# Own chunks first, weight loads in pairs over two rings, and the W_out casts on one engine: a change to the start of a convolution and GELU feed-forward kernel

## The chip, the cores and the metric

The kernel runs on one core of one Trainium2 chip. The metric is the device time of one execution in microseconds (us). The profile of a run shows a span that is about 1.7 us shorter than the run's time. Times below are medians of runs; positions inside a trace are us from the start of the span.

## The reference

Eight sequences of 4096 tokens with 192 channels go through a causal convolution of 7 taps. The taps are a softmax over a small weight table, one row for each of 8 heads of 24 channels. The result goes through a feed-forward layer with an exact GELU.

```python
def _attn_ref(x, weight):                 # x [8, 4096, 192], weight [8, 7]
    w = np.exp(weight - np.max(weight, axis=-1, keepdims=True))
    w = w / (np.sum(w, axis=-1, keepdims=True) + 1e-09)
    x_pad = np.concatenate([np.zeros((B, 6, D)), x], axis=1)
    ...                                   # idx: the 7 tokens that end at each token
    return np.einsum('hk,bskhg->bshg', w, x_unf).reshape(B, S, D)

def _moe_ref(x, w_in, w_out):             # w_in [192, 2048], w_out [2048, 192]
    h = x @ w_in
    g = 0.5 * h * (1.0 + erf(h * inv_sqrt2))
    return (g @ w_out).astype(np.float32)
```

## The kernel before

The 32768 tokens are split into two halves. Partitions 0 to 63 hold channels of half 0, partitions 64 to 127 those of half 1, so two products of 64 rows run side by side on TensorE (in the trace of this kernel the two of a pair start 3 ns apart at 32.14 us and take 269 ns each). Each half is cut into 35 blocks, of which the first six have 256 tokens and the others 512. Blocks 0 and 1 are convolved on TensorE, with diagonal tap matrices; VectorE convolves all later blocks. A small block is worked in 8 slices. A slice is 12 matmuls with W_in, one GELU of 1.02 us on ScalarE, and a share of the 128 matmuls with W_out that belong to the block before.

W_in arrives as float32. Half 0's partitions load the first 1024 columns and half 1's the last 1024. The "own" cast turns a group of 256 of these columns into bf16 on the partitions that loaded it. A "dup" copies a group to the other half's partitions, because each half of the tokens needs all 2048 columns. Loads are issued by SyncE (the "SP ring") and by ScalarE (the "ACT ring"); the page lists the two as queues q1 and q10, with 52.51 and 0.98 MB in this kernel.

```python
CH = []                                      # order of the 16 chunks of 128 columns, both halves alike
for s in range(4):
    CH += [2 * s, 2 * s + 1, NF // 2 + 2 * s, NF // 2 + 2 * s + 1]

def own(e, s):                               # f32 -> bf16, 128 partitions
    e.wait_ge(S_WIN[s], 32)
    ...
def dup(s, hf):                              # to the other half, 64 partitions, read from the f32 copy
    v.wait_ge(S_WIN[s], 32)
    ...
# VectorE, blocks 0 and 1
for p in range(NP):
    trans(0, p)
own(v, 0).then_inc(S_DUPE)
dup(0, 0)
conv_out(v, 0, 1)
conv_out(v, 0, 4)
dup(0, 1)
dup(1, 0)
dup(1, 1)
for p in range(NP):
    trans(1, p)
own(v, 2).then_inc(S_DUPE)
for s in (2, 3):
    for hf in range(2):
        dup(s, hf)
for j in range(len(PIECES)):
    conv_out(v, 1, j)
for i in range(2, 4):
    wcast(v, i).then_inc(S_WOC)

# TensorE, at the start of a slice of block 0
t.wait_ge(S_DUPE, (2, 3, 4, 5, 7, 8, 9, 10)[i])
t.wait_ge(S_OWN, sum(s <= i // 2 for s in OWNG))

# SP ring
load(sp, 0, (0, 1))
for s in range(2):
    win_in(sp, s, 0)                         # half 1 of these two groups goes out on ACT's ring
load(sp, 1)
for s in range(2, 4):
    for hf in range(2):
        win_in(sp, s, hf)
for i in range(4):
    wout_in(sp, i)
load(sp, 2)
```

## Time and profile before

| what | value |
|---|---|
| time, 3 runs | 687.38 us (687.08 to 687.88) |
| span of the profiled run | 684.6 us |
| TensorE busy | 675.7 us, 99% of the span |
| block 0's first product | 11.09 us |
| block 1's first product | 21.61 us |
| block 2's first product | 32.14 us |

Apart from the warm-up matmuls, TensorE does the same work in every version here, and from block 2 on it has no hole (busy for 645.7 of the 646 us from 34 to 680 us, before and after). So the time is the start of block 2's first product plus a constant: 684.6 − 32.14 = 652.5 us in this trace. Everything is decided in the first 33 us.

The timeline of TensorE in the kernel before shows how that time is spent. The columns are start, duration, engine, line, operation, tiles, shape and count; the bracket is the idle time before the group and what ended it.

```profile
11.09 4.51 PE L781 MATMUL hp<-xc,win 64*128 64x256 bf16 x48 [2.08 <-POOL win L226]
16.73 0.83 PE L781 MATMUL hp<-xc,win 64*128 64x256 bf16 x12 [1.13 <-ACT gT L703]
19.66 1.50 PE L781 MATMUL hp<-xc,win 64*128 64x256 bf16 x24
21.61 0.83 PE L781 MATMUL hp<-xc,win 64*128 64x256 bf16 x12 [0.45 <-ACT gT L703]
```

### The profile page before, as it was taken

The numbers are of one execution on the slowest core, as the hardware profiler recorded it, in microseconds if no ns is written. First come the engines' busy times: TensorE is split into PE (matmuls) and PEld (weight loads), VectorE is DVE, ScalarE is ACT, GpSimd is POOL, SyncE is SP. The second block draws the span as 40 slices with busy tenths as digits, with TensorE's granted clock in tenths as the row PEclk, the third lists the DMA queues.
The fourth block names the chain that finished last, engine by engine and source line by source line (L and its number), as shares of the span: only waits on it lengthen the run. The fifth ranks groups of instructions, "written<-read, shape, count | busy, mean of one in ns | idle before, by whom it ended". The sixth has DMA issues, their size and how long they took to land.

```text
span 684.6 us, 27324 instructions
## 1 busy us (share of the span) xinstructions
PE 675.7 (99%) x12576; PEld 408.9 (60%) x12576; DVE 564.1 (82%) x905; ACT 537.2 (78%) x550; POOL 35.9 (5%) x52
## 2 busy tenths in 40 slices
PE   6999999999999999999999999999999999999998
PEld 3899755555555555555555555555555555555557
DVE  6999989888898888898888898888898888988611
ACT  5899987877777877788777877777877777778772
POOL 3124200000000000000000000000000000000000
PEclk9999999999999999999999999999999999999999
DMA  9454421244422344422344322444322444221223
GB/s 231 87 116 109 103 60 35 62 94 95 94 60 59 73 94 95 93 57 53 83 94 95 88 51 56 91 94 95 81 48 63 95 94 95 69 48 29 48 49 94
DMA packets 134322, 55.23 MB, mean 81 GB/s; under 512 B 127552, under 2 KB 134208, under 8 KB 134208
## 3 DMA queue, kind: packets, MB, share of 16 engines
q1 hardware_dynamic: 132640, 52.51, 34.9%
q8 instruction: 98, 1.61, 1.0%
q10 hardware_dynamic: 1536, 0.98, 0.5%
q14 instruction: 16, 0.13, 0.1%
q0 software_dynamic: 32, 0.00, 0.0%
HBM read 28.31 MB, written 25.17 MB: 78 GB/s over the span
## 4 chain that ended last, share of the span: by engine, by line
PE 96%; ACT 2%; DMA 1%; issue 1%; DVE 0%; POOL 0%; ACTq 0%; POOLq 0%
PE hp L781 48%; PE ob L843 42%; PE ob L812 5%; ACT gT L703 2%; DMA winf<-in_moe_w_in_dram 1%; DMA wsb<-in_weight_dram 0%; PE ob L733 0%; ACT osb L301 0%; DVE osb L343 0%; POOL win L226 0%; DVE osb L312 0%; ACT L644 0%; ACT wex L637 0%; DVE wmx L490 0%; ACTq L238 0%
## 5 line engine op out<-in xcount | busy, mean ns | idle before, releaser
L703 ACT ACTIVATE gT<-hp 128x1024 bf16<-128x1024 f32 x512 | 523.4, 1024 | 131.5 <-PE hp L781 128.3
L781 PE MATMUL hp<-xc,win 64*64 64x512 bf16 (+2 forms) x6048 | 419.7, 367 | 3.8 <-POOL win L226 2.1
L843 PE MATMUL ob<-gT,wout 64*64 64x512 bf16 x5376 | 366.3, 376 | 0.0
L571 DVE SCALAR_TENSOR_TENSOR acc<-xT,wcol,acc 128x512 f32<-128x512 f32 (+1 forms) x495 | 314.6, 704 | 0.0
L781 PEld LDWEIGHTS hp<-xc,win 64*64 64x64 bf16 (+1 forms) x6048 | 189.0, 106 | 138.4 <-ACT gT L703 3.2
L843 PEld LDWEIGHTS ob<-gT,wout 64*64 64x64 bf16 x5376 | 172.2, 118 | 122.6
L343 DVE STREAM_TRANSPOSE osb<-ob 128x512 f32<-128x512 f32 x84 | 74.2, 886 | 102.0 <-PE ob L843 102.0
L538 DVE STREAM_TRANSPOSE xT<-xin 128x512 f32<-128x512 f32 (+1 forms) x105 | 78.0, 795 | 0.0
L571 DVE SCALAR_TENSOR_TENSOR xc<-xT,wcol,acc 128x512 bf16<-128x512 f32 (+1 forms) x99 | 65.2, 715 | 0.0
L471 POOL COPY xT<-xT 128x18 f32<-128x18 f32 x30 | 28.0, 934 | 509.0 <-DVE xT L538 486.6
L812 PE MATMUL ob<-wout,gT 64*128 64x192 bf16 x1024 | 51.8, 243 | 0.1
L812 PEld LDWEIGHTS ob<-wout,gT 64*128 64x128 bf16 x1024 | 43.7, 94 | 5.7 <-issue 0.4
L564 DVE TENSOR_SCALAR acc<-xT,wcol 128x512 f32<-128x512 f32 (+1 forms) x90 | 37.6, 474 | 1.1
L314 ACT ACTIVATE osb<-ob 128x192 f32<-128x192 f32 x4 | 1.3, 332 | 9.5 <-PE ob L812 9.5
L312 DVE COPY osb<-ob 128x192 f32<-128x192 f32 x4 | 1.4, 358 | 8.4 <-PE ob L812 8.4
L514 DVE CAST win<-winf 64x768 bf16<-64x768 f32 x8 | 6.6, 820 | 0.3
L717 PE MATMUL hp<-warm 128*128 128x512 bf16 x16 | 5.3, 505 | 1.3 <-DVE warm L487 1.3
L301 ACT ACTIVATE osb<-ob 128x384 f32<-128x384 f32 x12 | 5.8, 486 | 0.0
L676 ACT ACTIVATE acc<-xT,wcol 128x256 f32<-128x256 f32 (+1 forms) x9 | 5.2, 576 | 0.0
L717 PEld LDWEIGHTS hp<-warm 128*128 128x128 bf16 x16 | 1.9, 125 | 4.2 <-issue 2.2
L733 PE MATMUL ob<-xTb,dg 64*64 64x256 bf16 (+1 forms) x112 | 3.2, 245 | 0.8 <-ACT xTb L652 0.8
L733 PEld LDWEIGHTS ob<-xTb,dg 64*64 64x64 bf16 x112 | 2.6, 106 | 1.7 <-ACT xTb L652 1.3
(31 smaller groups left out, 21.3 us busy)
## 6 DMA issues: line engine op xcount, KB each, us to landing
out_dram<-osb SPq DMA_DIRECT2D x122, 192.0 KB, 3.6
xin<-in_x_dram SPq DMA_DIRECT2D x116, 192.0 KB, 4.2
xin<-in_x_dram SPq DMA_DIRECT2D x22, 96.0 KB, 3.9
woutf<-in_moe_w_out_dram SPq DMA_DIRECT2D x4, 384.0 KB, 7.5
winf<-in_moe_w_in_dram SPq DMA_DIRECT2D x6, 192.0 KB, 5.6
winf<-in_moe_w_in_dram ACTq DMA_DIRECT2D x2, 192.0 KB, 4.8
out_dram<-osb SPq DMA_DIRECT2D x8, 48.0 KB, 1.7
out_dram<-osb ACTq DMA_DIRECT2D x4, 96.0 KB, 2.0
```

What stands on the lines that cost most here:

```text
L343: v.transpose(ap(osb[m % 2], j, [[8 * C, 128], [C // 2, TB // 32], [NP, 32]]), bank(ring(m, j)),).then_inc(S_EV)
L471: g.tensor_copy(dst, src).then_inc(S_HALO)
L514: v.tensor_copy(ap(win, 64 * (1 - hf) * NP * F + FH + FP[s], [[NP * F, 64], [F, NP], [1, FP[s + 1] - FP[s]]],), ap(winf, 64 * hf * NP * FH ...
L538: v.transpose(ap(xT[n % 2], p * XW + HX, [[NP * XW, 128], [1, w]]), ap(xin[n % NX], p, [[TB // 32 * DQ, 128], [DQ, w // 32], [NP, 32]],),) ...
L564: ins = v.tensor_scalar(a, src, wk, None, ALU.mult)
L571: ins = v.scalar_tensor_tensor(dst, src, wk, a, op0=ALU.mult, op1=ALU.add)
L703: a.activation(out=ap(gT[n % 2], i * c * 2 * w, dst), in_=ap(hp[u % 2], 0, src), func=AF.Gelu,).then_inc(S_GELU)
L717: t.matmul(hp[1][:, 0:512], warm[:, 0:128], warm[:, :])
L733: ins = t.matmul(bank(kd, slice(64 * ho, 64 * ho + 64), w), dg[r, d0 : d0 + 64], xTb[PC[n]][r, x0 : x0 + w], start=(k == KS - 1), stop=(k ...
L781: ins = t.matmul(hp[u % 2][fo : fo + fw, o : o + w], ap(win, f1, [[NP * F, 64], [2, fw]]), xc[n % 2][r, p * TB : p * TB + w], start=(p == ...
L812: ins = t.matmul(bank(bb[sub], w=C), gT[m % 2][r, c0 : c0 + 128], wout[r, CH[i] * C : (CH[i] + 1) * C], start=(ph == 0 and i == 0), stop=( ...
L843: ins = t.matmul(bank(ring(m, j), slice(64 * h, 64 * h + 64), w), ap(wout, 64 * hf * NF * C + CH[i] * C + j, [[NF * C, 64], [NP, 64]],), g ...
```

## The change

The intent is to start TensorE earlier and to keep VectorE free for block 2.

1. Each half begins with the chunks of its own part of W_in: half 0 takes chunks 0 to 15, half 1 takes 8 to 15 and then 0 to 7. Slices 0 to 3 need only own casts, one on VectorE and three on GpSimd.
2. The dups read the bf16 copy, not the float32 one.
3. All W_in groups are loaded in pairs, half 0 on the SP ring and half 1 on ACT's ring, ahead of x block 1.
4. The softmax weights are loaded first on the SP ring, and no longer by GpSimd.
5. GpSimd casts all four pieces of W_out.
6. In block 1 the W_out matmuls are spread unevenly over the slices, and TensorE waits for the W_out casts at two named units (a unit is two W_out matmuls).

```diff
-    CH = []
-    for s in range(4):
-        CH += [2 * s, 2 * s + 1, NF // 2 + 2 * s, NF // 2 + 2 * s + 1]
+    CH = [[(8 * hf + i) % NF for i in range(NF)] for hf in range(2)]
 ... GpSimd
-            own(g, OWNG[0]).then_inc(S_OWN)
+            for s in range(1, 4):
+                own(g, s).then_inc(S_OWN)
             halo(1)
             for p in range(NP):
                 cast(g, 1, p)
-            own(g, OWNG[1]).then_inc(S_OWN)
-            for i in range(2):
+            for i in range(4):
                 wcast(g, i).then_inc(S_WOG)
 ... VectorE, in dup(s, hf)
-                v.wait_ge(S_WIN[s], 32)
+                if s == 0:
+                    v.wait_ge(S_DUPE, 1)
+                else:
+                    v.wait_ge(S_OWN, s)
 ...
-                        winf,
+                        win,
 ... VectorE
             own(v, 0).then_inc(S_DUPE)
-            dup(0, 0)
             conv_out(v, 0, 1)
             conv_out(v, 0, 4)
-            dup(0, 1)
-            dup(1, 0)
-            dup(1, 1)
+            for s in range(2):
+                for hf in range(2):
+                    dup(s, hf)
             for p in range(NP):
                 trans(1, p)
-            own(v, 2).then_inc(S_DUPE)
 ...
-            for i in range(2, 4):
-                wcast(v, i).then_inc(S_WOC)
 ... ScalarE
-            for s in range(2):
+            for s in range(4):
                 win_in(a, s, 1)
 ... TensorE
-                    t.wait_ge(S_DUPE, (2, 3, 4, 5, 7, 8, 9, 10)[i])
-                    t.wait_ge(S_OWN, sum(s <= i // 2 for s in OWNG))
+                    if 1 <= i < 4:
+                        t.wait_ge(S_OWN, i)
+                    else:
+                        t.wait_ge(S_DUPE, 1 if i == 0 else 2 * (i - 4) + 3)
 ...
+            share = {1: [4, 8, 8, 8, 9, 9, 9, 9]}
 ...
-                    ws = SHARE if new else [1] * NSL[n]
+                    ws = SHARE if new else share.get(n, [1] * NSL[n])
 ...
-                    if n == 1 and i < 2:
-                        t.wait_ge((S_WOG, S_WOC)[i], 2)
                     for un in todo[a0:a1]:
+                        if n == 1 and un in ((0, 0, 0), (0, 0, 4)):
+                            t.wait_ge(S_WOG, 2 + un[2] // 2)
 ... SP
+            sp.dma_start(wsb ...).then_inc(S_WSB, 16)     # taken from GpSimd
             load(sp, 0, (0, 1))
-            for s in range(2):
+            for s in range(4):
                 win_in(sp, s, 0)
             load(sp, 1)
-            for s in range(2, 4):
-                for hf in range(2):
-                    win_in(sp, s, hf)
```

More of the change, by code (lines that the diff above doesn't have):

```diff
@@ L152, in bass_lightweight_conv__then__act_gelu_exact_kernel @@
         S_OWN = sem("S_OWN")
-        S_WOC = sem("S_WOC")
         S_WOG = sem("S_WOG")
@@ L217, in bass_lightweight_conv__then__act_gelu_exact_kernel @@
         FP = [0, 256, 512, 768, FH]
-        OWNV = (0, 2)
-        OWNG = (1, 3)
         WG = [0, 4, 2, 6]
@@ L411, in _ @@
         def _(g):
-            g.dma_start(
-                wsb[:, :], ap(wt, 0, [[KS, H], [0, 64 // H], [1, KS]])
-            ).then_inc(S_WSB, 16)
             g.wait_ge(S_MSET, 1)
@@ L520, in dup @@
                     ap(
-                        winf,
-                        64 * hf * NP * FH + FP[s],
-                        [[NP * FH, 64], [FH, NP], [1, FP[s + 1] - FP[s]]],
+                        win,
+                        64 * hf * NP * F + FP[s],
+                        [[NP * F, 64], [F, NP], [1, FP[s + 1] - FP[s]]],
                     ),
@@ L594, in _ @@
             own(v, 0).then_inc(S_DUPE)
-            dup(0, 0)
             conv_out(v, 0, 1)
             conv_out(v, 0, 4)
-            dup(0, 1)
-            dup(1, 0)
-            dup(1, 1)
+            for s in range(2):
+                for hf in range(2):
+                    dup(s, hf)
             for p in range(NP):
                 trans(1, p)
-            own(v, 2).then_inc(S_DUPE)
-            for s in (2, 3):
+            for s in range(2, 4):
                 for hf in range(2):
@@ L766, in mm1 @@
                 if n == 0:
-                    t.wait_ge(S_DUPE, (2, 3, 4, 5, 7, 8, 9, 10)[i])
-                    t.wait_ge(S_OWN, sum(s <= i // 2 for s in OWNG))
+                    if 1 <= i < 4:
+                        t.wait_ge(S_OWN, i)
+                    else:
+                        t.wait_ge(S_DUPE, 1 if i == 0 else 2 * (i - 4) + 3)
                 for cc in range(c):
-                    f0 = 256 * (CH[i * c + cc] // 2) + CH[i * c + cc] % 2
                     for p in range(NP):
@@ L776, in mm1 @@
                             r = slice(64 * hf, 64 * hf + 64)
+                            ch = CH[hf][i * c + cc]
+                            f0 = 256 * (ch // 2) + ch % 2
                             fw = 64 if M0 < n <= M1 else 128
@@ L814, in mm2 @@
                         gT[m % 2][r, c0 : c0 + 128],
-                        wout[r, CH[i] * C : (CH[i] + 1) * C],
+                        wout[r, CH[sub][i] * C : (CH[sub][i] + 1) * C],
                         start=(ph == 0 and i == 0),
@@ L846, in mm2_t @@
                                 wout,
-                                64 * hf * NF * C + CH[i] * C + j,
+                                64 * hf * NF * C + CH[h][i] * C + j,
                                 [[NF * C, 64], [NP, 64]],
@@ L890, in _ @@
         def _(sp):
+            sp.dma_start(
+                wsb[:, :], ap(wt, 0, [[KS, H], [0, 64 // H], [1, KS]])
+            ).then_inc(S_WSB, 16)
             load(sp, 0, (0, 1))
-            for s in range(2):
+            for s in range(4):
                 win_in(sp, s, 0)
             load(sp, 1)
-            for s in range(2, 4):
-                for hf in range(2):
-                    win_in(sp, s, hf)
             for i in range(4):
```

## The prediction

> **What bounds the kernel now.** I read the busy times first, then the slices, then the first 35 us of the chain and of the engines' timelines.
>
> ```profile
> PE 675.7 (99%) x12576; PEld 408.9 (60%) x12576; DVE 564.1 (82%) x905; ACT 537.2 (78%) x550; POOL 35.9 (5%) x52
> ...
> PE   6999999999999999999999999999999999999998
> ...
> PEclk9999999999999999999999999999999999999999
> DMA  9454421244422344422344322444322444221223
> ```
>
> TensorE is busy for 99% of the span, at full granted clock, and only the first slice (17 us) has a hole. The change leaves the number and shape of matmuls alone, so it can only earn what TensorE loses at the start. The chain of waits shows that loss:
>
> ```profile
> 5.13 4.99 DMA winf<-in_moe_w_in_dram
> 10.12 0.05 issue
> 10.17 0.84 POOL win L226
> 11.01 0.09 issue
> 11.09 3.78 PE hp L781 x35
> ...
> 15.93 0.80 issue
> ...
> 21.61 0.83 PE hp L781 x12
> 22.44 0.66 PE ob L812 x16
> ```
>
> The first product with W_in (block 0) starts at 11.09 us, block 1's first product at 21.61. From there the stream has a period of 1.31 us per slice (12 matmuls with W_in, 16 with W_out) without a hole. The idle times in front of TensorE's instructions after the warm-up matmuls sum to 0.77 + 2.08 + 1.13 + 0.45 = 4.4 us; a stretch at reduced clock comes on top (granted clock 0.72 between 10 and 16 us). Note that the chain names GpSimd's cast of chunk 1 as the releaser at 11.09. The code says otherwise: the first slice waits for VectorE's duplicate (ended 10.53) and VectorE's copy of the convolution result (10.57 to 10.99), and that copy is the true releaser. Both sit behind VectorE's own cast, which waited for W_in until 9.13.
>
> VectorE has a second line to watch, since it computes the convolution for blocks 2 and on:
>
> ```profile
> 21.62 1.03 DVE L235 CAST wout<-woutf 128x768 bf16<-128x768 f32 x2
> 22.57 1.34 DVE L538 STREAM_TRANSPOSE xT<-xin 128x256 f32<-128x256 f32 x3
> ...
> 30.67 1.27 DVE L571 SCALAR_TENSOR_TENSOR xc<-xT,wcol,acc 128x256 bf16<-128x256 f32 x3
> ...
> 32.14 0.82 PE L781 MATMUL hp<-xc,win 64*128 64x256 bf16 x12
> ```
>
> VectorE works without a pause from 22.57 to 31.94 (9.4 us) on block 2, and TensorE takes that block at 32.14: a slack of 0.2 us. It is the same at block 3 (conv done 42.5, product at 42.66); from block 4 on, where ScalarE makes the first tap, the slack is 2 us and more. So **what TensorE gains before block 2 counts only as far as VectorE starts block 2 earlier too.** Two things hold that start: VectorE's earlier queue, and the landing of x block 2, whose last piece landed 9.3 us after an issue at 12.26, at 21.55.
>
> Last, what the DMA moved in three stretches (the last two columns are the share of the 16 engines and GB/s):
>
> ```profile
> 9.40:12.20 2.80, 1.11 (x14) 0.83 (x16) 2.67 (x6) 0.28 (x2) 0.98 (x2) 0.88 1.12 240
> 13.50:16.50 3.00, 2.10 (x26) 1.16 (x22) 2.97 (x5) 2.63 (x3) 2.51 (x5) 0.76 1.07 374
> 17.50:20.50 3.00, 3.00 (x86) 2.28 (x86) 2.84 (x6) 2.05 (x2) 0.84 (x2) 1.00 1.29 215
> ```
>
> The engines are saturated in all three, yet W_in pieces (64 partitions each, one after the other on one ring) move at 240 GB/s, W_out (128 partitions) at 374, x (32 partitions each) at 215.
>
> [...] from 4.4 to 5.0 us the SP ring wrote W_in to partitions 0 to 63 while the ACT ring finished x on 64 to 127, and 359 GB/s moved. That is one short stretch with mixed packet sizes. [...] The duplicates now read f32, and the shortest takes 684 ns for 768 elements; no bf16 copy is in this trace. [...] a duplicate takes 686 ns at the median and up to 1273 while GpSimd casts.
>
> **The change part by part.**
>
> *Softmax weights on the SP ring.* They land 2.8 us after a GpSimd issue at 1.32, at 4.13; issued first on SP at 0.81 I estimate 3.0, since the first 96 KB piece of x took 2.7 us. So the tap matrix is ready at about 5.2 instead of 6.34. x block 0 landed at 5.46 and its SP half now goes out 0.6 us later, so the transpose starts at about 5.5 instead of 6.25: 0.7 earlier. ScalarE's cast must stand behind four issues of 0.62 us from about 3.4 on, so it starts at about 6.0 instead of 6.86. The convolution on TensorE ends at about 8.2 instead of 9.0.
>
> *Own chunks first.* Slice 0 needs only one cast of chunk group 0 and no duplicate. Once the convolution copies are out (VectorE about 8.1) TensorE starts at about **8.4 instead of 11.09**. Slices 1 to 3 wait for GpSimd's three casts of 0.82 us.
>
> *Pairs over both rings.* Both halves of a chunk group fly together, ahead of x block 1. If the rate rises from 240 to 350 GB/s, W_in's 1.57 MB take 4.5 us instead of 6.5: groups land at about 6.5, 7.4, 8.4, 9.4 (x block 1 at about 11.2), and everything behind comes 2 us earlier. If not, they land at about 7.1, 8.7, 10.3, 11.9 and x block 1 where it landed before, 13.8.
>
> *Order of slices.* ScalarE's GELU takes 1.02 us, more than TensorE's 0.65 per slice, so slices follow at 1.03 us where weights allow. With the fast DMA: GELU of slice 0 at 9.2 to 10.2, slice 3 until 13.3. The four duplicates of groups 0 and 1 [...] and x block 1's transposes (1.35) end at about 13, the block-1 convolution on TensorE at 15.2, the last four duplicates at 15 to 16.6, VectorE's six copies (2.29 us) at 17.3 to 18.9. Block 1's first product then comes at **17.1 to 18.7 instead of 21.61**: 2.9 to 4.5 us gained on TensorE. With the slow DMA the same sum gives 19.7 to 20.6: 1.0 to 1.9.
>
> *W_out on GpSimd.* Four casts of 1.015 us from about 13.7 end at 17.7 to 19.6. They are needed after block 1's second slice (18.7 to 20.3), so they just fit. VectorE loses 1.03 us of casts before block 2.
>
> *VectorE's start of block 2.* It is the later of its copies (17.3 to 18.9) and x block 2. With the fast DMA I put x block 2 at 21.55 minus 2.4, so 19.1: 3.4 us earlier. With the slow DMA it lands at about 21.5, and the start moves from 22.57 to 21.6: 1.0 us.
>
> The gain is the smaller of the two lines: about **3.0 us** with the fast DMA (2.9 to 3.4), about **1.0 us** with the slow one. Steady state carries either shift unchanged to the end: its period is TensorE's own, and what is issued in it stays the same in number and shape.
>
> **The rivals.**
> *A: pairing does not raise the rate.* [...] Against: 359 GB/s in the one mixed stretch. Then x block 2 caps the gain: 687.4 − 1.0 = 686.4.
> *B: GpSimd becomes the bound.* It takes 3 + 4 casts (about 2.5 + 4.1 us) and three of block 1[...]. If its last W_out cast is a microsecond or two late, TensorE waits in block 1's second slice, and the gain falls to about 1: 686.4. For: the 1273 ns duplicate. Against: GpSimd is idle for over 5 us of the first 16 today.
> *C: TensorE stays cold.* Sparse matmuls brought the half clock from 11.5 to 14.9 today, after a 2.08 us hole. If slices 0 to 3 waited for weights, slices would take about 1.3 us, and about 0.5 to 1 us would be lost: 685.4.
> *D: nothing.* If some wait of block 1 that I have not seen holds its old time, 687.4. Slower than that would need a longer start, of which I see no sign.
>
> **Range and chances.** I give the fast DMA 65%, the slow 35%: 0.65 × 3.0 + 0.35 × 1.0 = 2.3, so 687.4 − 2.3 = **685.1**. The lower end, 683.8, is the fast case with both lines at their best (3.6); the upper, 686.8, is rival A or B with noise of 0.4 (the three runs before span 0.8). Two per cent is 13.7 us, more than the whole start holds to be won (11.09 before the first product), so faster 0.005, same 0.99, slower 0.005.
>
> **What would show it.** Right: first product near 8.4; W_in groups landing in pairs 0.9 us apart with over 330 GB/s in the stretch; [...] block 1's first product at 17 to 19; VectorE's transposes of block 2 starting when x lands, near 19; a gap of TensorE in front of block 2's first product if VectorE is the shorter line; identical busy time afterwards. Wrong: W_in at 240 GB/s (A), a TensorE wait for GpSimd at the first W_out matmuls (B), a granted clock of 0.5 past 10 us (C), or a new gap or a changed period after 35 us, which none of this holds.

The sum is 0.65 × 3.0 + 0.35 × 1.0 = 2.3 us gained, 687.4 − 2.3 = 685.1. The 350 GB/s of the fast case is an estimate from the 359 GB/s of the mixed stretch and the 374 of W_out. That sparse matmuls "brought" the half clock, in rival C, is a reading: the trace shows a granted clock of 0.50 from 11.5 to 14.9 us, after the hole of 2.08 us, and not what caused it. There a pair of products with W_in started every 213 ns instead of 109, which is the rival's 1.3 us per slice of six pairs instead of 0.65.

## The result, and the profile after

| | runs | median us | range |
|---|---|---|---|
| before, same rounds | 4 | 687.63 | 687.08 to 688.47 |
| changed | 4 | 686.32 | 686.22 to 687.87 |

The ratio is 0.9985 with a 95% interval of 0.9967 to 1.0003: the same within 2%, and not clear of zero. All ratios in this document are those of fast runs of the same rounds. They are close to the ratio of the means, and not quite the ratio of the medians quoted beside them.

The profiled run of the changed kernel was its slowest (687.87 us), and the profiled run of the kernel before was quicker than each of its timed runs. Read as a pair, the two profiles would say that the change loses 1.5 us. I therefore profiled each kernel again (runs r_before, r_after and r_after2 below) and use five traces.

The page of the changed kernel begins as follows: busy time of each engine, then busy tenths in 40 slices.

```profile
PE 676.0 (99%) x12576; PEld 408.4 (60%) x12576; DVE 561.1 (82%) x902; ACT 537.2 (78%) x550; POOL 37.0 (5%) x54
...
PE   7899999999999999999999999999999999999998
```

TensorE has the same matmuls and the same busy time within 0.3 us. VectorE lost 3.0 us of work, GpSimd gained 1.1. The first slice of TensorE rose from 6 to 7 tenths and the second fell from 9 to 8. What was gained in the first 17 us was handed back in the next 17. The chain of waits of the changed kernel names the places:

```profile
7.34 7.94 DMA xin<-in_x_dram
...
15.30 0.54 DVE xT L533
...
18.99 1.10 PE hp L774 x17
20.09 1.89 issue
...
26.18 0.05 issue
26.23 0.50 PE ob L805 x8
```

Before, the chain ran through W_in, by the group that landed at 10.12 us. Now it runs through x block 1, which lands at 15.28 us. Then TensorE stands still for 1.89 us **in the middle of a slice**, after 17 matmuls of a pair of slices, and no wait on a semaphore ends the stop; the profile calls it "issue". TensorE's timeline in the changed kernel shows the same stop with the holes before it:

```profile
10.38 0.87 PE L774 MATMUL hp<-xc,win 64*128 64x256 bf16 x12 [1.58 <-DVE xc L193]
12.00 0.83 PE L774 MATMUL hp<-xc,win 64*128 64x256 bf16 x12 [0.76 <-POOL win L222]
13.71 0.83 PE L774 MATMUL hp<-xc,win 64*128 64x256 bf16 x12 [0.88 <-POOL win L222]
14.87 1.61 PE L774 MATMUL hp<-xc,win 64*128 64x256 bf16 x24 [0.34 <-POOL win L222]
...
18.92 1.17 PE L774 MATMUL hp<-xc,win 64*128 64x256 bf16 x17
21.98 1.25 PE L774 MATMUL hp<-xc,win 64*128 64x256 bf16 x19 [1.89 <-issue]
...
33.71 0.82 PE L774 MATMUL hp<-xc,win 64*128 64x256 bf16 x12
```

Slices 1, 2 and 3 each wait for the next own cast on GpSimd, which waits for its W_in group. The granted clock stayed at 1.00, though; before, it had been 0.50 from 11.5 to 14.9 us. The pair of slices that began at 19.66 begins at 18.92. Block 2's first product, however, comes at 33.71 instead of 32.14.

The windows view of the changed kernel, over two stretches in which W_in moves and one in which W_out moves, has busy time and count of PE, PEld, DVE, ACT and POOL, then granted clock, DMA share and GB/s:

```profile
5.00:9.00 4.00, 3.80 (x64) 2.02 (x62) 1.79 (x4) 2.11 (x7) 1.03 (x3) 1.00 0.96 218
9.00:13.50 4.50, 1.70 (x24) 1.01 (x24) 3.00 (x7) 2.40 (x5) 1.67 (x2) 1.00 1.14 242
14.50:17.50 3.00, 2.62 (x54) 1.88 (x52) 2.14 (x5) 2.78 (x3) 1.98 (x6) 1.00 1.06 357
```

The same two W_in stretches in the kernel before:

```profile
5.00:9.00 4.00, 3.23 (x64) 1.96 (x61) 2.47 (x7) 3.12 (x7) 1.02 (x3) 1.00 1.16 230
9.00:13.50 4.50, 2.42 (x28) 1.71 (x28) 4.18 (x8) 1.68 (x4) 0.98 (x2) 0.78 1.12 242
```

Pairing did not raise the rate. The stretch from 5 to 9 us is no clean test, because in the kernel before groups 0 and 1 already went one half on each ring. From 9 to 13.5 us, where the kernel before loads mostly single pieces, the rate is 242, 254 and 232 GB/s in the three traces after and 242 and 246 in the two before. The fourth group of W_in lands at 13.85, 12.68 and 13.48 us (13.77 and 14.30 before).

VectorE's line shows what happened on the prediction's second line, VectorE's start of block 2:

```profile
22.87 1.34 DVE L533 STREAM_TRANSPOSE xT<-xin 128x256 f32<-128x256 f32 x3 [1.35 <-DMA xin<-in_x_dram]
```

VectorE was free 1.35 us earlier and waited for x block 2. Before, it began at 22.57 without a wait.

The five traces side by side, in us:

| | before | r_before | after | r_after | r_after2 |
|---|---|---|---|---|---|
| own cast of group 0 starts (VectorE) | 9.13 | 9.93 | 9.13 | 8.73 | 9.50 |
| first product | 11.09 | 11.90 | 10.38 | 9.98 | 10.75 |
| x block 1's transposes start (VectorE) | 13.38 | 14.19 | 15.30 | 14.40 | 14.88 |
| last pair of slices of block 0 starts | 19.66 | 20.47 | 18.92 | 18.03 | 18.50 |
| stop without a semaphore | none | none | 1.89 | 1.03 | 1.63 |
| block 1's first product | 21.61 | 22.42 | 22.32 | 20.57 | 21.65 |
| x block 2's transposes start (VectorE) | 22.57 | 23.38 | 22.87 | 21.97 | 22.74 |
| block 2's convolution ends (VectorE) | 31.94 | 32.75 | 32.25 | 31.34 | 32.11 |
| block 2's first product | 32.14 | 32.95 | 33.71 | 31.96 | 33.04 |
| span | 684.6 | 685.4 | 686.1 | 684.4 | 685.5 |

From own cast to first product it is 1.96 and 1.97 us before, and 1.25 us in all three traces after: the dup that left this path was worth 0.7 us. The last pair of slices starts at 20.07 on the mean before and at 18.48 after, a gain of 1.6 us. From there to block 1's first product it is 1.95 us before, and 3.40, 2.54 and 3.15 after. Block 1 itself takes 10.53 us before and 11.39 after. So of the gain of 1.6 us the stop takes back 0.6 to 1.5, and block 1 takes back 0.86. VectorE's line gained less: x block 2 landed at 22.85, 21.94 and 22.72 us (21.55 and 21.90 before), and block 2's convolution ended at 31.90 on the mean after and at 32.35 before, 0.45 us earlier.

### The profile page after: what moved, and what is told of

It reads as the page before. It is cut to its first block, busy times and chain, and to the rows that moved or that the text cites. A ratio compares the mean times of both kernels' runs of the same rounds, so it can differ in the third digit from the quotient of the medians.

```text
span 686.1 us, 27321 instructions
## 1 busy us (share of the span) xinstructions
PE 676.0 (99%) x12576; PEld 408.4 (60%) x12576; DVE 561.1 (82%) x902; ACT 537.2 (78%) x550; POOL 37.0 (5%) x54
## 3 DMA queue, kind: packets, MB, share of 16 engines
q8 instruction: 98, 1.61, 1.0%
## 4 chain that ended last, share of the span: by engine, by line
PE 95%; ACT 2%; DMA 1%; SPq 1%; issue 1%; DVE 0%; POOL 0%
PE hp L774 47%; PE ob L836 42%; PE ob L805 5%; ACT gT L694 1%; DMA xin<-in_x_dram 1%; SPq L355 0%; SPq L234 0%; PE ob L724 0%; ACT osb L297 0%; DVE osb L339 0%; POOL xTb L206 0%; SPq L888 0%; DVE xT L533 0%; DVE osb L308 0%
## 5 line engine op out<-in xcount | busy, mean ns | idle before, releaser
L509 DVE COPY win<-win 64x768 bf16<-64x768 bf16 x8 | 4.1, 515 | 0.8 <-POOL win L222 0.6
L231 POOL CAST wout<-woutf 128x768 bf16<-128x768 f32 x4 | 3.4, 882 | 0.5 <-DMA woutf<-in_moe_w_out_dram 0.5
```

## The experiments

**Theory and rivals after the result.** The theory: TensorE's start was gained, and two new costs in front of block 2 take it back. They are the stop after the 217th matmul (T) and the uneven share of block 1 (U). Rival S: the stop belongs to the place in the program, that is, to slice 8 and what it waits for. Rival L: nothing is handed back, the loads alone decide, and any order of them only changes which wait comes last.

About the stop the traces say two things more. It stands before the same matmul, the 218th, in each of the six traces that have the changed load order and 16 warm-up matmuls (1.0 to 2.0 us long in five of them, 0.21 us in e_128). And it ends shortly after a packet of 16 KB on the DMA queue that the profile labels "instruction": the packet ended at 20.48, 18.83 and 19.66 us in after, r_after and r_after2, and TensorE went on at 21.98, 20.23 and 21.31, which is 1.4 to 1.65 us later. In the kernel before, that packet ended at 16.93 and 17.51 us, well before TensorE got that far. Version T is an inference from these times: the stop is a wait for that packet, and the change delays it. What the packets hold, no trace shows. Their number goes with TensorE's work: in a whole run the pages show 98 such packets for 25,152 matmuls and weight loads of TensorE, one per 257, in all nine traces with 16 warm-ups, and 99 in all five traces of the 56-warm-up kernels below, which have 80 more of these instructions. That the stop is a wait for this packet is not shown by the count. The DMA view of the stretch of the stop (changed kernel, 18 to 20.6 us; packets, MB, share of 16 engines) has it once, beside 1319 packets of loads:

```profile
q8 instruction: 1, 0.02, 3.2%
```

### r_after and r_before: how much of it is noise

The edit is none: each kernel again as it is, five rounds.

> The changed kernel again, for the spread and a second trace. Theory 1 ([...] it is a matter of luck): in a run near 686.3 the hole is absent, TensorE's block 1 starts about 21.4 and the span is near 684.5; if the time is near 687.9, the hole is there again. Rival (the hole belongs to the changed order of work): it is there in every trace, whatever the time.

> The kernel before again, for a second trace, as its first trace (686.27) was below all of its timed runs (687.08 to 688.47). Theory 1: a run near 687.4 shows a hole of about 1 us of TensorE that no semaphore explains, which the first trace did not have; a run near 686.3 shows none. Rival: the first 35 us look the same and the difference lies elsewhere.

The hole of r_after's theory 1 is the stop of 1.89 us in the first trace, from 20.09 to 21.98 us.

| run | median us | before, same rounds | ratio (95%) |
|---|---|---|---|
| r_after, 6 runs | 687.23 (686.12 to 688.18) | 687.00 (11 runs) | 1.0000 (0.9988 to 1.0012) |
| r_before, 6 runs | 687.03 (686.47 to 688.75) | 687.00 (11 runs) | 1.0001 (0.9987 to 1.0014) |

Theory 1 fell in both: the profiled run of r_after, at 686.12 us, still had a stop (1.03 us), and that of r_before, at 687.10, had none. The stop belongs to the changed order. Runs of one kernel spread over 2 us, and in these rounds the change shows no gain. The traces (in the table above) show that the whole spread arises before block 2: the landing of W_in's first group alone moves by 0.8 us among the traces of each kernel.

### e_share: the even share back

```diff
-            share = {1: [4, 8, 8, 8, 9, 9, 9, 9]}
+            share = {}
```

> The changed kernel with the slices of block 1 given 8 W_out units each again, instead of 4, 8, 8, 8, 9, 9, 9, 9. In the trace of the changed kernel TensorE waits twice in block 1 (0.3 us start to start at 26.2 and 31.7) for its own last matmul, where a phase of 16 units ends inside a slice. Theory: both waits go, block 1 takes 10.5 us instead of 11.0, the kernel gains about 0.4 us on the changed one. Rival: the uneven split is needed since W_out's last cast comes late (21.1 us); then TensorE waits for GpSimd in block 1's first slice and the kernel loses up to 0.6 us.

Measured: 687.04 us (5 runs, 685.94 to 687.70) against 687.00, ratio 0.9995 (0.9982 to 1.0008). In the trace block 1 takes 10.58 us instead of 11.39. In the changed kernel two groups of W_out matmuls are split by a short wait, at 26.23 us (in the chain above) and at 31.73; each lengthens its group by 0.24 us. The first slice of block 1 has only 8 W_out matmuls, so TensorE stands until the GELU is done, another 0.38 us. The three sum to the 0.86 us; none of them is in this trace. So cost U is real: 0.8 us of TensorE's time in block 1. The traces show it: in this one and in the first trace of the changed kernel the last pair of slices began at 18.92 us, and block 2's first product came at 32.99 instead of 33.71, although the stop was a little longer (1.97 against 1.89). The times can't resolve it: r_after, in the same rounds, had 687.23, and runs of one kernel spread over 2 us. The rival's wait for GpSimd did not come.

### e_128: W_in in DMAs over all 128 partitions

Each W_in group as one DMA over all 128 partitions. W_in does not lie in that shape, so this run loads other bytes of the same size (from x): its **result is wrong** (relative error 1.71). ACT's four issues fall away with it.

```diff
 # own(): one DMA per group
-            e.wait_ge(S_WIN[s], 32)
+            e.wait_ge(S_WIN[s], 16)
 # win_in(): 128 partitions at once, bytes of x
+                ap(winf, FP[s], [[NP * FH, 128], [FH, NP], [1, FP[s + 1] - FP[s]]]),
+                ap(xt, FP[s], [[NP * F, 128], [F, NP], [1, FP[s + 1] - FP[s]]]),
 # ScalarE
-            for s in range(4):
-                win_in(a, s, 1)
```

> The changed kernel, but each group of W_in is one DMA over all 128 partitions on the SP ring, with the same packet size (1 KB) and the same pitch in DRAM, taken from x: the result is wrong on purpose, the work is the same. Theory A [...]: W_in moves at about 350 GB/s, its last group lands near 9.5 us instead of 13.8, x block 2 near 20 instead of 22.9, TensorE's block 1 starts 2 us or more earlier and the kernel gains 1.5 to 3 us on the changed one. Theory B [...]: W_in stays at 200 to 260 GB/s and the time stays within 0.5 us.

No run here shows either, so the causes are cut and the forecasts stand.

Measured: 686.58 us (5 runs, 685.98 to 687.25) against 687.00, ratio 0.9993 (0.9981 to 1.0005). The windows view of this run:

```profile
5.00:9.00 4.00, 3.36 (x67) 2.07 (x65) 3.69 (x9) 3.08 (x9) 1.35 (x4) 1.00 0.94 287
9.00:13.50 4.50, 2.06 (x36) 1.48 (x32) 2.03 (x4) 2.20 (x3) 1.32 (x2) 1.00 1.10 231
```

The rate in the first stretch is 287 GB/s against 218 in the first trace of the changed kernel (238 and 225 in the other two), and the first product came at 8.76 us. The fourth group still landed at 13.46 us, against 13.85, 12.68 and 13.48. Its packets on 15 of the 16 DMA engines had ended by 12.3 us; those of one engine ended over 1 us later. Even this shape therefore gains nothing clear for the later groups, and slices 2 and 3 wait (TensorE idle 2.27 us before 12.86, clock at half from 14.66, and 0.53 granted on the mean from 14.5 to 17.5). The step "pairing makes 350 GB/s" was not only wrong for pairs; a single DMA of 128 partitions did not reach it either.

### e_more: 56 short warm-up matmuls in place of 16 long ones

This moves the 218th matmul to an earlier point of the program without changing any load. The columns of the warm-up stay alike (56 × 146 = 8176, 16 × 512 = 8192); it took 5.10 us in this trace, and with 16 matmuls 5.30 (before), 6.23 (after), 5.08 (r_after) and 6.57 us (e_unpair).

```diff
-            for i in range(16):
-                t.matmul(hp[1][:, 0:512], warm[:, 0:128], warm[:, :])
+            for i in range(56):
+                t.matmul(hp[1][:, 0:146], warm[:, 0:128], warm[:, 0:146])
```

> The changed kernel with 56 warm-up matmuls of 146 columns instead of 16 of 512: the same columns, 40 more pairs of weight load and matmul ahead of everything. In four traces of changed kernels TensorE stopped, with no semaphore to wait for, before its 218th matmul (22.0, 20.2, 22.1 and 21.2 us), 1.4 to 1.5 us after the first 16 KB packet on the instruction queue had ended. Theory F [...]: the stop comes before the 218th matmul again, now 40 matmuls earlier in the work (in the second half of the block-1 convolution instead of the eighth slice), or there is no stop [...]. Rival S (the stop belongs to the eighth slice, for a wait that the trace does not show): it stays in the eighth slice, before its sixth matmul.

Theory F, called the instruction theory in later runs, is version T: the stop is a wait for the packet.

Measured: **686.08 us** (4 runs, 685.96 to 686.57) against 687.05, ratio 0.9985 (0.9970 to 1.0000). The stop is gone, as TensorE's timeline of this run shows:

```profile
19.09 1.49 PE L774 MATMUL hp<-xc,win 64*128 64x256 bf16 x24
21.04 0.39 PE L774 MATMUL hp<-xc,win 64*128 64x256 bf16 x4 [0.46 <-ACT gT L694]
...
32.42 0.82 PE L774 MATMUL hp<-xc,win 64*128 64x256 bf16 x12
```

The last pair of slices runs through (x24, not x17 and x19), and block 1 starts 1.95 us after it, exactly as in the kernel before. Rival S falls: slice 8 waits for the same things as before the edit. The 16 KB packet now ended at 17.28 us. What is shown is that the stop goes when 40 more, and narrower, matmuls stand ahead: none of the four traces with 56 warm-ups on top of the changed kernel has it. That the stop is a wait for the packet is an inference from the times and the count; the trace does not tell what a packet holds. One time fits less well: here TensorE passed the 218th matmul 1.23 us after the packet had ended, without a stop, while the stops ended 1.35 to 1.65 us after it.

### e_hold: does the packet stand behind x block 3?

SP waits for eight slices before it issues x block 3, so the rings are emptier when the packet is due.

```diff
             load(sp, 2)
+            sp.wait_ge(S_MM1, 8)
             load(sp, 3)
```

> The changed kernel with the SP queue waiting for TensorE's eighth slice before it issues the loads of x block 3 and later. Theory Q ([...] in the changed kernel SP's issues of x blocks 2 to 4 take about 1 us each from 14 to 19 us): the first instruction packet starts 2 us or more earlier (near 16 us instead of 17.6 to 19.2), the 1.3 to 2.2 us stop of TensorE before the 218th matmul goes, and x block 2 lands up to 1 us earlier. Rival [...]: the packet still starts after 17.5 us and the stop stays.

Theory Q has the packet stand behind the data loads; the rival has its time follow TensorE's progress.

Measured: 687.37 us (4 runs, 686.14 to 688.63) against 687.05, ratio 1.0003 (0.9984 to 1.0021). The stop was still there, 1.25 us, and the packet ended at 21.27. My guess that the packet stood behind the loads of x block 3 and later is refuted; W_out and x block 2 were still in flight (they landed until 20.55 and 21.63 us). In this trace TensorE was also at half clock from 11.04 to 17.86 us, with holes of 1.93, 0.40 and 0.27 us in front of the slices.

### e_unpair: the changed kernel with the load order of before

```diff
 # ScalarE
-            for s in range(4):
+            for s in range(2):
                 win_in(a, s, 1)
 # SP
-            for s in range(4):
+            for s in range(2):
                 win_in(sp, s, 0)
             load(sp, 1)
+            for s in range(2, 4):
+                for hf in range(2):
+                    win_in(sp, s, hf)
```

> The changed kernel with W_in issued as in the kernel before (groups 0 and 1 one half on each ring, x block 1, then groups 2 and 3 on SP alone). Theory A (a pair in flight moves no faster than one piece after the other): group 3 lands as before, at 13 to 14 us, x block 1 about 3 us earlier than in the changed kernel (10.6 instead of 13.8 to 15.3), slices 2 and 3 start within 0.7 us of the changed kernel's, and the time is within 0.7 us of it. Theory P (pairing helps): group 3 lands 1.5 us or more later and the third and fourth slices start that much later.

Measured: **688.39 us** (4 runs, 687.82 to 689.18) against 687.05, ratio 1.0015 (0.9998 to 1.0031). TensorE's timeline of this run:

```profile
10.57 1.52 PE L774 MATMUL hp<-xc,win 64*128 64x256 bf16 x24 [1.44 <-DVE xc L193]
14.63 1.47 PE L774 MATMUL hp<-xc,win 64*128 64x256 bf16 x12 [2.53 <-POOL win L222]
16.42 2.74 PE L774 MATMUL hp<-xc,win 64*128 64x256 bf16 x24 [0.33 <-POOL win L222]
```

With own chunks first and the old load order, slices 2 and 3 want groups 2 and 3, which stand behind x block 1; group 3 lands at 15.40 us. TensorE waits 2.53 us, and its clock falls to half from 14.09 to 20.9 us. The new load order is thus worth 1.4 to 2.1 us to the new slice order (the range is from the difference to e_unpair's own rounds of before plus the pooled gain given below, to its distance from the official median), by order and not by rate: 225 GB/s moved from 9 to 13.5 us. Part of it is the clock: the pair of slices at 16.42 took 2.74 us, against 1.49 to 1.61 at full clock in the three traces of the changed kernel, and all four runs of e_unpair have a mean granted clock of 0.994 to 0.998. Theory A's forecast (group 3 at 13 to 14 us, the time within 0.7) missed; theory P's came, group 3 1.6 to 2.7 us later, but through the order. There was no stop without a semaphore in this trace; the packet ended at 19.68 and TensorE reached the 218th matmul later. Counted from TensorE's 120th matmul, the packet started 0.2 to 0.9 us later with the old load order (three traces with 16 warm-ups) and 3.1 to 3.9 us later with the new one (six). So, against TensorE's progress, the new load order delays the packet. By the clock alone it does not: here it started at 18.35 us, and at 17.61 to 19.15 in the three traces of the changed kernel. That TensorE's progress is the right thing to count from is my assumption, and why the packet is late stays open.

### e_moreshare: e_more and e_share together

> The changed kernel with the 56 narrow warm-up matmuls (which took the stop before the 218th matmul away) and with 8 W_out units in each slice of block 1. In the trace of the 56-matmul kernel block 2's first product (32.42) came 0.25 us after VectorE's convolution of block 2 (32.17), which had started at 22.77, as the last piece of x block 2 landed. Theory C (VectorE's start, set by x block 2's landing, is the cap): taking the two phase waits out of block 1 (0.5 us) gains less than 0.3 us; block 2's first product stays 0.2 us behind VectorE's convolution, which ends 9.4 us after x block 2 has landed. Rival (TensorE's own work is the bound): the kernel gains 0.5 us on the 56-matmul kernel (686.1), and block 2's first product comes 0.5 us or more after the convolution.

Measured: 686.25 us (5 runs, 685.58 to 686.74) against 686.89, ratio 0.9987 (0.9974 to 0.9999). First TensorE, then VectorE, in this run:

```profile
32.11 0.82 PE L774 MATMUL hp<-xc,win 64*128 64x256 bf16 x12
```

```profile
22.29 1.35 DVE L533 STREAM_TRANSPOSE xT<-xin 128x256 f32<-128x256 f32 x3 [0.55 <-DMA xin<-in_x_dram]
...
30.40 1.27 DVE L566 SCALAR_TENSOR_TENSOR xc<-xT,wcol,acc 128x256 bf16<-128x256 f32 x3
```

With the stop and the uneven share both gone, block 2's first product (32.11) follows VectorE's last convolution instruction (ended 31.67) by 0.44 us, and VectorE had waited for x block 2. The two lines of the prediction, TensorE's and VectorE's, lie close together here. In e_more they were 0.25 us apart, in the kernel before 0.2. This would explain why taking away the share as well gave nothing that the times show: VectorE, and behind it the landing of x block 2, stands close behind TensorE. The 0.44 us lies between the two forecasts (0.2, and 0.5 or more), so neither is confirmed.

### e_x2: x block 2 ahead of the last two W_out pieces

On top of e_moreshare, x block 2 is issued before the last two pieces of W_out, and block 0's W_out matmuls first use the two pieces that come early.

```diff
-            for i in range(4):
+            for i in range(2):
                 wout_in(sp, i)
             load(sp, 2)
+            for i in range(2, 4):
+                wout_in(sp, i)
             load(sp, 3)
```

> As e_moreshare, but x block 2 is loaded ahead of the last two pieces of W_out, and block 0's W_out units take chunk groups 0 and 1 of either half first, so that the first 8 need only the first two pieces. Theory C: x block 2 lands near 20 us instead of 22 to 23, VectorE starts block 2 at 20.5 to 21, block 2's first product moves from about 32.3 to 30.5 to 31.3, and the time from 686.1 to 684.5 to 685.3. Rival D (the last W_out piece becomes the bound): it lands at 21 to 22.5, TensorE waits for GpSimd's cast in block 1's second slice, and the time stays at 686 or more.

Measured: 686.85 us (5 runs, 685.86 to 687.29) against 686.89, ratio 0.9997 (0.9983 to 1.0011). VectorE started block 2 at 19.86 us, 2.4 us earlier than in e_moreshare, and the cap was lifted. In its place TensorE waited for W_out:

```profile
20.99 0.82 PE L774 MATMUL hp<-xc,win 64*128 64x256 bf16 x12
23.06 0.83 PE L805 MATMUL ob<-wout,gT 64*128 64x192 bf16 x16 [1.25 <-POOL wout L231]
```

GpSimd's cast of the last piece ran from 22.18 to 23.00, as soon as the piece had landed. Rival D held. That is the prediction's rival B in its form, but the cause is the load, not GpSimd, which had been idle for 1.07 us.

### v_best: the same loads with a finer order of the W_out matmuls

On top of e_x2, TensorE does all that the two early pieces of W_out allow, for both groups of 128 tokens, before it touches the late ones.

```diff
+                    parts = [(0, 0, lo), (1, 0, lo), (0, 0, hi), (0, 1, al), (1, 0, hi), (1, 1, al)]
```

> As e_x2, whose TensorE stopped for 1.25 us at 21.8 us for the cast of the last W_out piece (ended 23.0), but block 0's W_out units run in an order that needs the last two pieces 8 units later: both groups' first halves, then the second halves. If the cap theory is right [...]: the stop shrinks from 1.25 to under 0.4 us, block 2's first product comes at 30.4 to 31.0 instead of 31.6, 0.2 us after VectorE's convolution, and the time is 684.6 to 685.4. If W_out's last piece lands a microsecond later again, 686.

The cap theory has the start set by when x block 2 and W_out's last piece land, not by how much any engine does.

Measured: 686.90 us (6 runs, 686.49 to 687.38) against 687.27, ratio 0.9991 (0.9977 to 1.0006). The wait for W_out was gone, but in this trace x block 1 landed late (its transposes began after 16 us), block 1 began at 21.91, and block 2's convolution ended at 32.60, 0.15 us before its first product at 32.75. VectorE had waited 0.88 us within this convolution for a small copy of GpSimd, which stood behind GpSimd's last W_out cast (24.38 to 25.21 us; the piece had landed at 24.33). So the late W_out pieces still cost time, now by way of VectorE. The forecast of 684.6 to 685.4 us missed. The kernel is no better than e_more. I had hoped for a version clearly ahead of both kernels and did not get one.

### r_after2: the changed kernel a third time, beside v_best

> The changed kernel a third time, beside the version that should beat it: 686.2 to 687.9, with a stop before TensorE's 218th matmul of 0.3 to 2.2 us in the trace, again 1.3 to 1.6 us after the first instruction packet ended. If the stop is absent or stands elsewhere, the instruction theory falls.

Measured: 686.66 us (5 runs, 686.30 to 687.28) against 687.27, ratio 0.9989 (0.9975 to 1.0004). The stop was 1.63 us long, before the 218th matmul, and ended 1.65 us after the packet (forecast: 1.3 to 1.6).

### c_before56: the control for e_more

The kernel before with the 56 short warm-up matmuls, to see whether these help by themselves.

> A control: the kernel before with the same 56 narrow warm-up matmuls. It had no stop before its 218th matmul, so if the instruction theory is right the 40 added pairs take nothing away there: its time stays within 0.4 us of the kernel before, and block 2's first product stays 0.2 us behind VectorE's convolution. Rival (narrow warm-ups help by themselves[...]): it gains 0.7 us or more, as the changed kernel did with them (686.1 and 686.2 against 686.9).

Measured: 687.28 us (6 runs, 686.40 to 688.70) against 687.05, ratio 1.0004 (0.9991 to 1.0016). They do not, in the kernel before: block 2's first product again came 0.2 us after VectorE's convolution. It fits that e_more gained by losing the stop, but e_more and the changed kernel never ran in the same rounds, so this is not shown by the times.

### All runs together

The 15 runs of the changed kernel have a mean of 686.92 us, all 59 runs of the kernel before one of 687.28: the change gains about 0.4 us, with an uncertainty of about the same size. The 9 runs of e_more and e_moreshare have a mean of 686.17, some 0.75 us below the changed kernel's. These pools mix rounds and chips, so they are weaker than the ratios; they only sum up.

## Why the prediction was right or wrong

**The time.** Predicted 685.1 us with a range of 683.8 to 686.8. The official median was 686.32, inside the range, near its upper part; over all 15 runs it is 686.92, just outside. That the number fell inside is thus partly luck of the four runs drawn, and the 2.3 us that were its middle were not reached. The expected gain was 2.3 us; the measured one is 1.3 by the official medians and 0.4 over all runs. "Within 2%" was right.

**What bounds the kernel**: right. Time follows block 2's first product with a constant of 652.4 to 652.5 us in all traces, and the steady state did not change. VectorE stayed within 0.2 us of TensorE in the kernel before, as read there.

**The step that failed** is "the rate rises from 240 to 350 GB/s, W_in's 1.57 MB take 4.5 us instead of 6.5", to which I had given 65%. The runs show 218 and 242 GB/s, and W_in landed at 9.1, 11.0, 12.7 and 13.85 us in the first trace (8.7, 9.9, 11.2 and 12.7 in the quickest), not at 6.5, 7.4, 8.4 and 9.4. I had built it on one stretch of 0.6 us with mixed packets, in which 359 GB/s moved. The trace before held a better test than that stretch: groups 0 and 1 already went one half on each ring there, and landed at 9.10 and 10.12 us. Even my slow case was too quick, with 7.1 to 11.9 us.

**The first product** was predicted at 8.4 and came at 9.98 to 10.75. The own cast waited for W_in's first group, at 8.7 to 9.5 us, about as long as before (9.1 and 9.9). Of the removed work only the dup's 0.7 us counted. The earlier softmax weights were on no critical path: they landed at about 3.4 (predicted 3.0), the transposes began at 5.47 (predicted 5.5), but the convolution was ready before W_in was. They also had a price: their issue took SP 0.80 us, the first W_in load was issued at 3.03 instead of 2.22, and in the first 5 us the DMA moved 91 to 93 GB/s instead of 120 and 121. I had counted this delay for x block 0 alone. No run takes part 4 out, so what it costs is not shown.

**x block 1.** In the slow case I left it "where it landed before, 13.8". That was a misreading: before, it landed at 10.59 us, and at 13.77 the last W_in group did. It now stands behind all of W_in, landed at 15.28, 14.38 and 14.86 us, and its transposes began at 14.40 to 15.30 us (13.38 and 14.19 before). VectorE waited 1.6 to 2.5 us for it. The intervening work of VectorE had shrunk by enough to absorb this: the last pair of slices still began 1.6 us earlier.

**x block 2**, the other end of the sum, was mis-sized too. The slow case had it at about 21.5 us and VectorE's start 1.0 us earlier. It landed at 22.85, 21.94 and 22.72 us, and VectorE's start moved from 22.98 to 22.53 on the mean, 0.45 us. (The fast case moved it by 2.4 us, though the prediction's own times for W_in, 6.5 and 4.5 us, give 2.0.)

**The dups** read bf16 now and took 418 ns at least, 421 at the median and 803 at most in the first trace (up to 956 in r_after); from float32 it had been 684, 686 and 1273 ns before. The longest of either trace (at 17.57 and at 15.35) ran beside casts of GpSimd throughout, yet one at 17.12, also beside GpSimd throughout, took 421 ns.

**Block 1's first product** at 19.7 to 20.6 in the slow case: measured 20.57, 21.65 and 22.32. The difference is the stop of 1.0 to 1.9 us, which the prediction did not have. I could not have read it in the profile before, since it does not occur there.

**Rival A** (no higher rate) happened, and its 686.4 was met by the official median. But its reason, that x block 2 caps the gain, is not what bounded these traces: the convolution of block 2 ended 1.46, 0.62 and 0.93 us before the product. TensorE's stop and the uneven share came first; e_more shows that the cap stands 0.25 us behind them. So the number was right and its working was not.

**Rival B** (GpSimd the bound) did not happen in the changed kernel: its last W_out cast ended at 21.14 us, before TensorE wanted it, in block 1's second slice at 24.35. A wait for GpSimd's casts appeared in e_x2 and, through VectorE, in v_best, both times behind the load.

**Rival C** (half clock) did not occur in the three traces of the changed kernel, and full clock there is probably part of the gain of 1.6 us, since the trace before has 3.4 us at a clock of 0.50; it occurred in e_hold, e_unpair, e_128 and e_more. Holes of 2.08 us (before), 2.53 (e_unpair) and 1.93 (e_hold), with sparse slices around them, stood beside 3.4, 6.8 and 6.8 us at half clock, while the three traces of the changed kernel kept full clock, with a hole of 2.00 us in r_after2. So the length of the hole alone does not tell. The clock of each run says more: traces with a stretch at half clock have a mean of 0.995 to 0.998 and those without one 0.999 or 1.000. Of the 15 runs of the changed kernel 5 lie at 0.998 or below, of the kernel before 47 of the 55 for which the clock is recorded. So the half clock became rarer and did not go. Runs without it are 0.4 us quicker on the mean in either kernel, so it may be part of the 0.4 us gained; no run separates it.

**The uneven share**: I did not price part 6 at all. It cost 0.86 us of TensorE's time in block 1.

**What stays open.** Why the 16 KB packet comes about 3 us later, by TensorE's progress, with the new load order; whether the stop is a wait for it, and what it holds (known is only that 98 such packets come with 25,152 of TensorE's instructions, and 99 with 80 more); and how much of the share's cost would show in the time if x block 2 landed earlier.

## What to carry to other kernels

If two lines stand 0.2 us apart at the end of a start-up phase, a gain on one of them alone is worth little, and reordering loads may only swap which piece is last: here it was x block 2 in e_moreshare and W_out's last piece in e_x2, and the 4.3 MB of W_in, W_out and three blocks of x had landed by 21.55 to 22.85 us in the five traces of the two kernels. Order loads by the consumer's order (e_unpair: 1.4 us or more), but test before you count on two DMAs to different partitions being quicker than one after the other: here they were not (232 to 254 GB/s in pairs, 242 and 246 for mostly single pieces). When TensorE stops in mid-slice and the profile names no releaser, count which matmul it is and look at the packets on the DMA queue that the profile labels "instruction" (here one of 16 KB ended 1.35 to 1.65 us before TensorE went on); and profile each kernel more than once when the effect is under a microsecond.
